# Attention chunks with one-bank accumulators, a third of the squares moved to ScalarE, and another order of the loads and copies around them

## The chip, the cores and the metric

The kernel runs on one core of one Trainium2 chip. The metric is the device time of one execution in microseconds, as the median of three runs. The engines are named as the profile names them: PE is the matrix engine (TensorE), PEld its weight loads, DVE is VectorE, ACT is ScalarE, POOL is GpSimd, SP is the engine that issues most of the DMAs.

## What is computed

```python
scores = (1.0 / S) * np.matmul(z, z.transpose(0, 2, 1))   # B=2, S=3008, d_qk=64
attn = np.maximum(scores, 0.0) ** 2
x = (u * np.matmul(attn, v)).reshape(B * S, D)            # D=256
for w_in, w_out in ((moe_w_in, moe_w_out), (moe2_w_in, moe2_w_out)):   # 256 -> 2048 -> 256
    h = x @ w_in
    g = h - np.tanh(h)      # first network
    # second network: g = h where h >= 1, 0 where h <= -1, (h + 1)**2 / 4 between
    x = g @ w_out
```

The weights come as 64-bit floats; u, v and z are 32-bit.

## The kernel before

Every product is made in three parts. A tile is kept as hi (the float rounded to the format that PE multiplies) and lo (what is left), and hi by hi, hi by lo and lo by hi are summed in PSUM.

**Attention.** For each batch the 3008 queries are cut into chunks of 512 columns (five, and a last one of 448), and the keys into 12 blocks of 256 (NPA). One step is one chunk and one block; there are 144 steps. In a step `attn_s` makes the scores on PE (6 matmuls into the tile `sc`, two banks), ACT takes them out with Relu and the factor 1/S (`r`, L260), DVE squares them in full precision (`a`, L267), ACT squares them rounded (`hi`, L268), and DVE subtracts (`lo`, L272). Two steps later (LAG) `attn_av` multiplies v by hi and lo: 24 matmuls, 20 in the last step of a chunk, in pairs of half the rows, h=0 and h=1, into two accumulators `acc[0]` and `acc[1]`. Each accumulator is a tile of two banks, one bank for each half d of the 256 columns of v, and the pool `ps_a` holds two such tiles, so that PSUM is full (`ps_s` has the other four banks). In the last step of a chunk the half d=0 is finished first: ACT copies `acc[0]`'s part to `y` (L309), DVE adds `acc[1]`'s (L310); then the same for d=1; at the end DVE multiplies by u (L315).

**Networks.** 12 chunks of 512 tokens, 8 blocks of 256 hidden columns each, twice. `ffn_s` makes 12 matmuls, ACT and DVE make g and split it, and two steps later `ffn_av` makes 12 more into an accumulator tile of two banks from `ps_a`. The last chunk of the second network is made untransposed and goes out by one ACT copy and one DMA.

**Loads.** z, v and the weights are loaded into four `raw` buffers, split into hi (ACT, L88) and lo (DVE, L91) and kept in a ring of 18 tiles; z is first transposed by DVE (L124). `pump(i)` issues the DMAs up to 14 steps ahead and the splits two steps ahead or when there is room. The weights are first turned from 64-bit to 32-bit floats by some seven DVE passes a tile (`convert`), dealt out by `make(i)` at CONVERT passes a step: 1.2 in the attention, 2.0 in the networks, and none in the first 12 steps and around the change of batch.

**Order.** The schedule is written out by hand: each engine works off its instructions in the order in which the code issues them, and waits only for the tiles that it reads or overwrites. The order of a step i is `pump(i)`, the hooks (u's loads and transposition), the scores and squares of step i, the deferred lo splits (`flush`), the product with v of step i-2, `make(i)`. So the copies y of a finished chunk, which belong to the product of step i-2, stand on ACT and DVE behind the squares of step i.

Of the kernel before, what the change touches and what calls it, by code (L numbers as in the profile page):

```python
# [15 lines left out]
P = 128  # L16
LAG = 2
GROUP = 1
# [5 lines left out]
CONVERT = (1.2, 2.0)  # L24
# [3 lines left out]
def attention_then_two_ffn(  # L28
# [15 lines left out]

    nc = tc.nc
# [8 lines left out]
    SCALE = 1.0 / S  # L54
# [12 lines left out]
    ps_a = ctx.enter_context(tc.tile_pool(name="ps_a", bufs=2, space=bass.MemoryType.PSUM))  # L67
# [33 lines left out]
    def load_z(b, g):  # L101
# [4 lines left out]
        def dma():  # L106
# [132 lines left out]
    accs = {}  # L239

    def attn_s(todo):

        got = []
        for b, c, t in todo:
            n = min(QT, S - QT * c)
            ps = ps_s.tile([P, 2, 512], F32, tag="s", name="sc")
            q = zs[b, c]
            for k, (x, y) in enumerate(((0, 0), (0, 1), (1, 0))):
                for j in range(2):
                    half = slice(64 * j, 64 * j + 64)  # L250
                    g, k0 = divmod((2 * t + j) * P, QT)
                    nc.tensor.matmul(  # L252
                        ps[:, j, :n], zs[b, g][half, x, k0 : k0 + P], q[half, y, :n], start=(k == 0), stop=(k == 2)
                    )
            got.append((ps, n))
        out = []
        for ps, n in got:
            s = (slice(None), slice(None), slice(0, n))
            r = tmp_p.tile([P, 2, 512], F32, tag="t1", name="r")
            nc.scalar.activation(out=r[s], in_=ps[s], func=AF.Relu, scale=SCALE)  # L260
            out.append((r, s, n))
        held = []
        for r, s, n in out:
            a = tmp_p.tile([P, 2, 512], F32, tag="t2", name="a")
            hi = sp_p.tile([P, 2, 512], F32R, tag="hi", name="hi")
            lo = sp_p.tile([P, 2, 512], F32R, tag="lo", name="lo")
            nc.vector.tensor_tensor(out=a[s], in0=r[s], in1=r[s], op=ALU.mult)  # L267
            nc.scalar.activation(out=hi[s], in_=r[s], func=AF.Square)  # L268
            held.append((hi, lo, n))
            got.append((a, s))  # L270
        for (a, s), (hi, lo, _) in zip(got[len(held):], held):
            nc.vector.tensor_tensor(out=lo[s], in0=a[s], in1=hi.bitcast(F32)[s], op=ALU.subtract)  # L272
        flush()
        return held

    def attn_av(b, c, t, hi, lo, n):
        if t == 0:
            accs[b, c] = [ps_a.tile([P, 2, 512], F32, tag="acc", name=f"acc{h}") for h in range(2)]
# [27 lines left out]
        for d in range(2):  # L306
            his(d)
            los(d)
            nc.scalar.activation(out=y[:, d, :n], in_=acc[0][:, d, :n], func=AF.Copy)  # L309
            nc.vector.tensor_tensor(out=y[:, d, :n], in0=y[:, d, :n], in1=acc[1][:, d, :n], op=ALU.add)  # L310
        o = 0
        while o < n:
            g, r = divmod(b * S + QT * c + o, 4 * P)
            k = min(n - o, 4 * P - r)
            nc.vector.tensor_tensor(  # L315
                out=xs[g][:, :, r : r + k], in0=y[:, :, o : o + k], in1=ut[:, :, o : o + k], op=ALU.mult
            )
            o += k
# [42 lines left out]
    def ffn_av(net, c, f, hi, lo, n):  # L361
        if f == 0:
            accs[net, c, "f"] = ps_a.tile([P, 2, 512], F32, tag="acc", name="acc")
# [221 lines left out]
```

## Time and profile before

| what | value |
|---|---|
| median of 3 runs | 1607.31 us (1605.94 to 1611.07) |
| the profiled execution | 1606.49 us |
| its span, first to last instruction | 1604.7 us |
| busy share of the span: PE, DVE, ACT | 96%, 71%, 48% |
| mean granted clock of PE | 0.98 of full speed |
| PE waiting for anything, by the list of waits | some 56 us, 41.5 of them for y (L309, L310) |

The share of busy time is a mean over stages with different limits: PE is busy without a break in the networks and has gaps in the attention. So the profile is read by stretches of the span, cut where chunks begin, then by what PE waited for, then as a timeline around a wait. A start in a timeline is where an instruction began, in us from the span's start; the bracket at the end of a row says how long the engine stood idle before it and which instruction let it go. The granted clock (PEclk) is 1.00 at 2.4 GHz and 0.50 at 1.2 GHz.

### The profile page before, as it was taken

The page shows a single profiled execution, that of the slowest core. Times are in us where ns is not written, and L with a number is a line of the kernel's source. Part 1 is how long each engine was busy: PE and PEld are TensorE (multiplying, and loading weights), DVE is VectorE, ACT ScalarE, POOL GpSimd, SP SyncE. Part 2 cuts the span into 40 slices and gives each one's busy share as a digit, 9 for nine tenths or more (in the row PEclk, how much of TensorE's full clock was granted, in tenths as well). Part 3 has the DMA queues.
Part 4 walks back from the last instruction along what each step waited for, and adds up shares of the span by engine and source line. Part 5 has one row for each costly group of instructions (what it writes and reads, how often), then busy time and mean ns, then how long its engine had stood idle before and what let it go on. Part 6 is the DMA issues. An engine that isn't in the chain of part 4 may idle for free.

```text
span 1604.7 us, 21195 instructions
## 1 busy us (share of the span) xinstructions
PE 1544.3 (96%) x8935; PEld 1300.1 (81%) x8935; DVE 1142.6 (71%) x1175; ACT 776.2 (48%) x806; POOL 0.7 (0%) x5
## 2 busy tenths in 40 slices
PE   7899999799999989999999999999999999999998
PEld 5677878688878868888888888898888888888888
DVE  6788888888888876666666544557776767767775
ACT  5555555655565744444444444445434344444443
POOL 0000000000000000000000000000000000000000
PEclk9899999899999999999999999999999999999999
DMA  4220223301211321111100000011000000000001
GB/s 108 57 60 21 54 56 76 86 17 41 57 35 46 104 72 40 40 40 40 37 23 27 33 1 0 14 30 37 13 13 14 14 14 13 12 4 13 14 14 24
DMA packets 146608, 56.70 MB, mean 35 GB/s; under 512 B 123600, under 2 KB 130128, under 8 KB 146512
## 3 DMA queue, kind: packets, MB, share of 16 engines
q1 hardware_dynamic: 146512, 55.34, 13.9%
q8 instruction: 70, 1.15, 0.3%
q14 instruction: 26, 0.21, 0.0%
HBM read 40.76 MB, written 14.55 MB: 34 GB/s over the span
## 4 chain that ended last, share of the span: by engine, by line
PE 89%; DVE 6%; ACT 2%; issue 1%; DMA 1%; SPq 1%; DVEq 0%
PE acc L370 31%; PE acc L287 21%; PE h L338 11%; PE h L340 11%; PE h L339 11%; PE sc L252 5%; DVE a L267 2%; DVE lo L272 1%; PE acc L403 1%; ACT r L260 1%; DMA zraw<-in_z_dram 1%; DVE y L310 1%; DVE v L91 1%; SPq L113 0%; DVE zt L124 0%
## 5 line engine op out<-in xcount | busy, mean ns | idle before, releaser
L287 PE MATMUL acc<-hi,v 64*128 64x512 f32 (+1 forms) x2256 | 328.9, 398 | 46.1 <-ACT y L309 27.1
L370 PE MATMUL acc<-gh,w_out 128*128 128x512 f32 (+1 forms) x1472 | 360.3, 387 | 0.0
L88 ACT ACTIVATE gh<-g 128x1024 fp32r<-128x1024 f32 (+1 forms) x192 | 200.4, 1044 | 267.6 <-DVE g L357 141.5
L287 PEld LDWEIGHTS acc<-hi,v 64*128 64x128 f32 x2256 | 253.1, 191 | 91.9 <-ACT y L309 32.8
L370 PEld LDWEIGHTS acc<-gh,w_out 128*128 128x128 f32 x1472 | 275.6, 188 | 54.7
L338 PE MATMUL h<-xl,w_in 128*128 128x512 f32 (+1 forms) x768 | 296.3, 386 | 0.0
L340 PE MATMUL h<-xh,w_in 128*128 128x512 f32 (+1 forms) x768 | 296.0, 385 | 0.0
L339 PE MATMUL h<-xh,w_in 128*128 128x512 f32 (+1 forms) x768 | 295.9, 385 | 0.0
L91 DVE TENSOR_TENSOR gl<-g,gh 128x1024 fp32r<-128x1024 f32 (+1 forms) x192 | 230.0, 1198 | 61.6 <-ACT gh L88 61.6
L349 DVE TENSOR_TENSOR g<-h,t 128x1024 f32<-128x1024 f32 (+1 forms) x96 | 115.4, 1203 | 149.5 <-ACT t L347 149.5
L352 DVE TENSOR_SCALAR t<-h 128x1024 f32<-128x1024 f32 (+1 forms) x96 | 115.4, 1203 | 142.1 <-PE h L340 142.1
L260 ACT ACTIVATE r<-sc 128x1024 f32<-128x1024 f32 (+1 forms) x144 | 145.0, 1007 | 144.3 <-PE sc L252 143.4
L370 PE MATMUL acc<-gl,w_out 128*128 128x512 f32 (+1 forms) x736 | 195.0, 387 | 0.0
L267 DVE TENSOR_TENSOR a<-r 128x1024 f32<-128x1024 f32 (+1 forms) x144 | 172.5, 1198 | 27.0 <-ACT r L260 26.0
L287 PE MATMUL acc<-lo,v 64*128 64x512 f32 (+1 forms) x1152 | 190.6, 392 | 0.5 <-DVE lo L272 0.5
L272 DVE TENSOR_TENSOR lo<-a,hi 128x1024 fp32r<-128x1024 f32 (+1 forms) x144 | 173.3, 1203 | 19.5 <-PE acc L287 1.0
L347 ACT ACTIVATE t<-h 128x1024 f32<-128x1024 f32 (+1 forms) x96 | 96.9, 1009 | 166.9 <-PE h L340 166.8
L355 ACT ACTIVATE t<-t 128x1024 f32<-128x1024 f32 (+1 forms) x96 | 100.3, 1045 | 156.5 <-DVE t L352 156.5
L338 PEld LDWEIGHTS h<-xl,w_in 128*128 128x128 f32 x768 | 144.6, 188 | 28.7 <-issue 0.6
L339 PEld LDWEIGHTS h<-xh,w_in 128*128 128x128 f32 x768 | 144.6, 188 | 27.7
L340 PEld LDWEIGHTS h<-xh,w_in 128*128 128x128 f32 x768 | 144.4, 188 | 27.5
L370 PEld LDWEIGHTS acc<-gl,w_out 128*128 128x128 f32 x736 | 137.9, 188 | 27.4
(52 smaller groups left out, 1078.2 us busy)
## 6 DMA issues: line engine op xcount, KB each, us to landing
wide_in<-in_moe_w_in_dram SPq DMA_DIRECT2D x16, 512.0 KB, 3.8
wide_out<-in_moe_w_out_dram SPq DMA_DIRECT2D x16, 512.0 KB, 3.9
vraw<-in_v_dram SPq DMA_DIRECT2D x22, 256.0 KB, 3.0
out_dram<-ot SPq DMA_DIRECT2D x88, 64.0 KB, 1.9
ub<-in_u_dram SPq DMA_DIRECT2D x80, 64.0 KB, 2.5
w_in<-m_in SPq DMA_DIRECT2D x16, 256.0 KB, 2.1
w_out<-m_out SPq DMA_DIRECT2D x16, 256.0 KB, 2.1
wraw_in<-w_in SPq DMA_DIRECT2D x16, 256.0 KB, 2.6
```

Source lines behind the costliest of these rows:

```text
L88: nc.scalar.activation(out=hi, in_=src, func=AF.Copy)
L91: nc.vector.tensor_tensor(out=lo, in0=src, in1=hi.bitcast(F32), op=ALU.subtract)
L260: nc.scalar.activation(out=r[s], in_=ps[s], func=AF.Relu, scale=SCALE)
L267: nc.vector.tensor_tensor(out=a[s], in0=r[s], in1=r[s], op=ALU.mult)
L272: nc.vector.tensor_tensor(out=lo[s], in0=a[s], in1=hi.bitcast(F32)[s], op=ALU.subtract)
L287: nc.tensor.matmul(acc[h][:, d, :n], lhsT, g[half, j, :n], start=start, stop=stop)
L338: nc.tensor.matmul(ps[:, j, :n], w[:, 0, k, fs], xl[:, k, :n], start=(k == 0), stop=False)
L339: nc.tensor.matmul(ps[:, j, :n], w[:, 1, k, fs], xh[:, k, :n], start=False, stop=False)
L340: nc.tensor.matmul(ps[:, j, :n], w[:, 0, k, fs], xh[:, k, :n], start=False, stop=(k == 1))
L349: nc.vector.tensor_tensor(out=g[s], in0=ps[s], in1=t1[s], op=ALU.subtract)
L352: nc.vector.tensor_scalar(out=t1[s], in0=ps[s], scalar1=1.0, scalar2=-1.0, op0=ALU.min, op1=ALU.max)
L370: nc.tensor.matmul(acc[:, d, :n], w[:, part, j, d * P : (d + 1) * P], g[:, j, :n], start=start, stop=stop)
```

## The change

The accumulators become tiles of one bank each: four for an attention chunk (`acc[d][h]`), two for a network chunk, out of a pool of four. The lo passes go to a list `tail` that is issued at the end of a step, behind the product with v and behind `make`; in step 1 of a chunk, which is the step in which the chunk before is finished, hi goes there too. In every third step (t % 3 == 2) the square `a` is made by ACT. The multiplication by u is deferred to the next step. The score factor leaves the Relu: z is scaled by 2**-6 when it is split, and the rest, squared, is applied with u. The conversion rate in the attention is 1.5 a step, with a longer pause around the change of batch and one around the end of the attention; the load splits are limited to one early step a time in the last chunk. At the start the loads of the first z go half to SP and half to ACT, only z is split before the first scores, and v's second block is loaded after the first step's scores are issued. The copies out of network accumulators are made bank by bank, the last one half on DVE and half on ACT with a DMA each.

```diff
-GROUP = 1
+ZEXP = 2.0**-6
...
-CONVERT = (1.2, 2.0)
+CONVERT = (1.5, 2.0)
...
-    SCALE = 1.0 / S
+    SCALE = (1.0 / S / ZEXP**2) ** 2
...
-    ps_a = ctx.enter_context(tc.tile_pool(name="ps_a", bufs=2, space=bass.MemoryType.PSUM))
+    ps_a = ctx.enter_context(tc.tile_pool(name="ps_a", bufs=4, space=bass.MemoryType.PSUM))
...
-        def dma():
+        def dma(other=nc.sync):
...
-                nc.sync.dma_start(
+                (other if i % 2 else nc.sync).dma_start(
...
-            split(w[:, 0, :], w[:, 1, :], zt, now=True)
+            nc.scalar.activation(out=w[:, 0, :], in_=zt, func=AF.Copy, scale=ZEXP)
+            nc.vector.scalar_tensor_tensor(
+                out=w[:, 1, :], in0=zt, scalar=ZEXP, in1=w[:, 0, :].bitcast(F32), op0=ALU.mult, op1=ALU.subtract
+            )
...
-            nc.scalar.activation(out=r[s], in_=ps[s], func=AF.Relu, scale=SCALE)
...
+    tail = []
...
+        nc.scalar.activation(out=r[s], in_=ps[s], func=AF.Relu)
+
+        def square_hi():
+            nc.scalar.activation(out=hi[s], in_=r[s], func=AF.Square)
+
+        if t % 3 == 2:
+            square_hi()
+            nc.scalar.activation(out=a[s], in_=r[s], func=AF.Square)
+        else:
             nc.vector.tensor_tensor(out=a[s], in0=r[s], in1=r[s], op=ALU.mult)
-            nc.scalar.activation(out=hi[s], in_=r[s], func=AF.Square)
-            held.append((hi, lo, n))
-            got.append((a, s))
-        for (a, s), (hi, lo, _) in zip(got[len(held):], held):
-            nc.vector.tensor_tensor(out=lo[s], in0=a[s], in1=hi.bitcast(F32)[s], op=ALU.subtract)
+
+            tail.append(square_hi) if t == 1 else square_hi()
         flush()
-        return held
+        tail.append(lambda: nc.vector.tensor_tensor(out=lo[s], in0=a[s], in1=hi.bitcast(F32)[s], op=ALU.subtract))
+        return hi, lo, n
...
-            accs[b, c] = [ps_a.tile([P, 2, 512], F32, tag="acc", name=f"acc{h}") for h in range(2)]
+            accs[b, c] = [[ps_a.tile([P, 512], F32, tag="acc", name=f"acc{d}{h}") for h in range(2)] for d in range(2)]
...
-                nc.tensor.matmul(acc[h][:, d, :n], lhsT, g[half, j, :n], start=start, stop=stop)
+                nc.tensor.matmul(acc[d][h][:, :n], lhsT, g[half, j, :n], start=start, stop=stop)
...
-            nc.scalar.activation(out=y[:, d, :n], in_=acc[0][:, d, :n], func=AF.Copy)
-            nc.vector.tensor_tensor(out=y[:, d, :n], in0=y[:, d, :n], in1=acc[1][:, d, :n], op=ALU.add)
-        o = 0
-        while o < n:
-            g, r = divmod(b * S + QT * c + o, 4 * P)
-            k = min(n - o, 4 * P - r)
-            nc.vector.tensor_tensor(
-                out=xs[g][:, :, r : r + k], in0=y[:, :, o : o + k], in1=ut[:, :, o : o + k], op=ALU.mult
-            )
-            o += k
+            nc.scalar.activation(out=y[:, d, :n], in_=acc[d][0][:, :n], func=AF.Copy)
+            nc.vector.tensor_tensor(out=y[:, d, :n], in0=y[:, d, :n], in1=acc[d][1][:, :n], op=ALU.add)
+
+        def scaled():
+            o = 0
+            while o < n:
+                g, r = divmod(b * S + QT * c + o, 4 * P)
+                k = min(n - o, 4 * P - r)
+                nc.vector.scalar_tensor_tensor(
+                    out=xs[g][:, :, r : r + k], in0=y[:, :, o : o + k], scalar=SCALE, in1=ut[:, :, o : o + k],
+                    op0=ALU.mult, op1=ALU.mult,
+                )
+                o += k
+
+        deferred.append(scaled)
...
-                nc.scalar.activation(out=xs[c], in_=acc[:, :, :n], func=AF.Copy)
+                for d in range(2):
+                    nc.scalar.activation(out=xs[c][:, d, :], in_=acc[d][:, :n], func=AF.Copy)
...
+                for d in range(2):
+                    nc.vector.transpose(out=o[:, d].rearrange("p c e -> p (c e)"), in_=acc[d])
...
+        for i, (t0, k) in enumerate(((0, min(2, nt)), (2, nt - 2))):
+            if k <= 0:
+                continue
+            src = acc[i][:, : k * D].rearrange("p (t d) -> p t d", d=D)
+            if i:
+                nc.scalar.activation(out=o[:, t0 : t0 + k, :], in_=src, func=AF.Copy)
+                nc.scalar.dma_start(out=to[:, t0 : t0 + k, :], in_=o[:, t0 : t0 + k, :])
+            else:
+                nc.vector.tensor_copy(out=o[:, t0 : t0 + k, :], in_=src)
+                nc.sync.dma_start(out=to[:, t0 : t0 + k, :], in_=o[:, t0 : t0 + k, :])
...
-                if i > 5 and ld in staged and ld["at"] < i - 1 and n < 2:
+                if i > 5 and ld in staged and ld["at"] < i - 1 and n < (1 if NATT - NPA <= i < NATT else 2):
...
+        first[0]["steps"][0][0](nc.scalar)
+        first[1]["steps"][0][0]()
+        warm(WARM)
+        first[0]["steps"][1][0]()
...
-        warm(WARM)
-        for ld in first:
-            ld["steps"][1][0]()
...
-        flush()
...
+        pauses = ((0, NPA), (NPA * QC - 9, NPA * QC + 13), (NATT - 5, NATT + 1))
...
+            if not any(a <= i < e for a, e in pauses):
+                state["credit"] += CONVERT[0] if i < NATT else CONVERT[1]
...
+        def second(i):
+            if i >= LAG:
+                _, av_fn, args = pairs[i - LAG]
+                av_fn(*args, *held.pop(i - LAG))
...
+            if i == LAG:
+                second(i)
...
-            for i in group:
-                if i >= LAG:
-                    _, av_fn, args = pairs[i - LAG]
-                    av_fn(*args, *held.pop(i - LAG))
-                make(i)
+            if i == 0:
+                first[1]["steps"][1][0]()
+                first[2]["steps"][0][0]()
+            elif i == 1:
+                first[2]["steps"][1][0]()
+            if i != LAG:
+                second(i)
+            make(i)
+            for fn in tail:
+                fn()
+            tail.clear()
 
 
 # ---- launch: one core; inputs and outputs as the reference has them ----
```

Three places show how rows move. First ACT and DVE where the first chunk of batch 0 ends: acc is the finished accumulator, e and m are conversion steps, x is the product with u; of the two r's the later one is of step 1 of the next chunk. ACT before, then after:

```order
L260 ACTIVATE r_684<-sc_677 128x1024
L268 ACTIVATE hi_687<-r_684 128x1024
L260 ACTIVATE r_728<-sc_721 128x1024
L268 ACTIVATE hi_731<-r_728 128x1024
L309 ACTIVATE y_736<-acc0_208 128x512 x2
L260 ACTIVATE r_770<-sc_763 128x1024
L268 ACTIVATE hi_773<-r_770 128x1024
```

```order
L264 ACTIVATE r_689<-sc_679 128x1024
L267 ACTIVATE hi_687<-r_689 128x1024
L264 ACTIVATE r_733<-sc_723 128x1024
L313 ACTIVATE y_736<-acc00_191 128x512
L313 ACTIVATE y_736<-acc10_193 128x512
L267 ACTIVATE hi_731<-r_733 128x1024
L264 ACTIVATE r_775<-sc_765 128x1024
L267 ACTIVATE hi_773<-r_775 128x1024
L271 ACTIVATE a_772<-r_775 128x1024
```

The two y copies stand ahead of hi_731 now, and the next step has a third pass, a_772. DVE at the same place, before, then after:

```order
L267 TENSOR_TENSOR a_686<-r_684 128x1024
L272 TENSOR_TENSOR lo_688<-a_686,hi_687 128x1024
L192 TENSOR_SCALAR e0_in_0_719<-wide0_in_0_716 128x512
L267 TENSOR_TENSOR a_730<-r_728 128x1024
L272 TENSOR_TENSOR lo_732<-a_730,hi_731 128x1024
L310 TENSOR_TENSOR y_736<-y_736,acc1_209 128x512 x2
L315 TENSOR_TENSOR x0_90<-y_736,ut0_0_589 128x1024
```

```order
L273 TENSOR_TENSOR a_686<-r_689 128x1024
L197 TENSOR_SCALAR e0_in_0_720<-wide0_in_0_717 128x512
L277 TENSOR_TENSOR lo_688<-a_686,hi_687 128x1024
L273 TENSOR_TENSOR a_730<-r_733 128x1024
L314 TENSOR_TENSOR y_736<-y_736,acc01_192 128x512
L314 TENSOR_TENSOR y_736<-y_736,acc11_194 128x512
L199 TENSOR_SCALAR m0_in_0_719<-wide0_in_0_717 128x512
L203 TENSOR_SCALAR e0_in_0_720<-e0_in_0_720 128x512
L277 TENSOR_TENSOR lo_732<-a_730,hi_731 128x1024
L321 SCALAR_TENSOR_TENSOR x0_90<-y_736,ut0_0_591 128x1024
```

The additions stand directly behind a_730, and lo_732 behind them and two conversion steps. Second, the start on ACT, before, then after (z0_0, v0_0: batch 0, first tile):

```order
L88 ACTIVATE z0_0_125<-zt0_0_123 128x512
L88 ACTIVATE v0_0_128<-vraw0_0_111 128x512
L88 ACTIVATE v0_1_130<-vraw0_1_113 128x512
L88 ACTIVATE z0_1_150<-zt0_1_148 128x512
L260 ACTIVATE r_160<-sc_153 128x1024
L268 ACTIVATE hi_163<-r_160 128x1024
L260 ACTIVATE r_177<-sc_170 128x1024
L268 ACTIVATE hi_180<-r_177 128x1024
```

```order
L115 DMA zraw0_0_106<-in_z_dram 32x16x32 x2
L128 ACT_TABLE_LOAD
L128 ACTIVATE z0_0_123<-zt0_0_121 128x512
L128 ACTIVATE z0_1_142<-zt0_1_140 128x512
L264 ACTIVATE r_155<-sc_145 128x1024
L267 ACTIVATE hi_153<-r_155 128x1024
L90 ACTIVATE v0_0_159<-vraw0_0_111 128x512
L264 ACTIVATE r_176<-sc_166 128x1024
L90 ACTIVATE v0_1_180<-vraw0_1_161 128x512
L267 ACTIVATE hi_174<-r_176 128x1024
```

The first r has no v ahead of it any more, and the second hi has v0_1 ahead of it. SP issues that v0_1 (vraw0_1) before, then after:

```order
L113 DMA zraw0_0_106<-in_z_dram 32x16x32 x4
L139 DMA vraw0_0_111<-in_v_dram 128x2x256
L139 DMA vraw0_1_113<-in_v_dram 128x2x256
L113 DMA zraw0_1_134<-in_z_dram 32x16x32 x4
L139 DMA vraw0_2_139<-in_v_dram 128x2x256
```

```order
L115 DMA zraw0_0_106<-in_z_dram 32x16x32 x2
L144 DMA vraw0_0_111<-in_v_dram 128x2x256
L115 DMA zraw0_1_126<-in_z_dram 32x16x32 x4
L144 DMA vraw0_2_131<-in_v_dram 128x2x256
L144 DMA vraw0_3_133<-in_v_dram 128x2x256
L115 DMA zraw0_2_135<-in_z_dram 32x16x32 x4
L144 DMA vraw0_1_161<-in_v_dram 128x2x256
```

Its issue has moved behind two v blocks and the third z.

## Rows read from the trace of the kernel before

**Rows 1.** Stretches: length; busy us and instructions of PE, PEld, DVE, ACT, POOL; PEclk, DMA, GB/s.

```profile
0.00:67.15 67.15, 52.65 (x365) 38.47 (x366) 49.74 (x55) 40.48 (x50) 0.73 (x5) 0.90 0.44 99
67.15:247.49 180.34, 168.90 (x1424) 141.53 (x1425) 153.45 (x167) 104.30 (x104) 0.00 (x0) 0.98 0.19 45
158.54:203.18 44.64, 41.71 (x357) 36.86 (x357) 38.82 (x43) 26.19 (x26) 0.00 (x0) 1.00 0.20 48
247.49:342.09 94.60, 81.54 (x712) 72.13 (x712) 81.13 (x93) 58.97 (x72) 0.00 (x0) 0.95 0.28 63
342.09:526.14 184.05, 173.41 (x1425) 151.16 (x1425) 153.42 (x171) 104.28 (x104) 0.00 (x0) 0.94 0.17 42
526.14:583.19 57.05, 50.67 (x391) 43.12 (x391) 48.15 (x64) 32.07 (x41) 0.00 (x0) 0.91 0.35 101
583.19:1604.70 1021.51, 1017.09 (x4621) 853.68 (x4619) 656.68 (x629) 436.06 (x435) 0.00 (x0) 1.00 0.08 22
```

**Rows 2.** What PE waited for: us in total, times, longest us.

```profile
PE acc L287 <- ACT y L309: 27.1, 12, 6.7
PE acc L287 <- DVE y L310: 14.4, 14, 2.1
```

**Rows 3.** Chain of waits, pace of PE (attention, then first network): start, us, what.

```profile
211.13 2.72 PE acc L287 x24
...
616.00 2.72 PE acc L370 x12
```

**Rows 4.** Timeline at one chunk boundary: start, us, engine, line, out<-in, [idle before].

```profile
155.89 1.03 ACT L260 ACTIVATE r<-sc 128x1024 f32<-128x1024 f32 x1 [1.28 <-PE sc L252]
156.15 0.83 PE L287 MATMUL acc<-lo,v 64*128 64x512 f32 x4
156.95 1.06 ACT L268 ACTIVATE hi<-r 128x1024 fp32r<-128x1024 f32 x1
156.95 1.23 DVE L267 TENSOR_TENSOR a<-r 128x1024 f32<-128x1024 f32 x1 [0.48 <-ACT r L260]
157.91 0.58 ACT L309 ACTIVATE y<-acc 128x512 f32<-128x512 f32 x1
158.31 1.23 DVE L272 TENSOR_TENSOR lo<-a,hi 128x1024 fp32r<-128x1024 f32 x1
158.54 0.50 PE L287 MATMUL acc<-hi,v 64*128 64x512 f32 x1 [1.56 <-ACT y L309]
159.45 0.68 DVE L310 TENSOR_TENSOR y<-y,acc 128x512 f32<-128x512 f32 x1
160.19 0.96 PE L287 MATMUL acc<-hi,v 64*128 64x512 f32 x5 [1.15 <-DVE y L310]
```

**Rows 5.** Timeline where batch 0 gives way to batch 1.

```profile
250.01 0.98 PE L252 MATMUL sc<-z,z 64*128 64x448 f32 x6
...
288.62 0.70 DVE L124 STREAM_TRANSPOSE zt<-zraw 128x512 f32<-128x512 f32 x1
289.36 0.63 ACT L88 ACTIVATE z<-zt 128x512 fp32r<-128x512 f32 x1 [3.47 <-DVE zt L124]
289.90 1.01 ACT L260 ACTIVATE r<-sc 128x1024 f32<-128x1024 f32 x1
294.94 0.53 ACT L309 ACTIVATE y<-acc 128x448 f32<-128x448 f32 x1
297.68 0.62 DVE L310 TENSOR_TENSOR y<-y,acc 128x448 f32<-128x448 f32 x1
301.29 0.91 PE L287 MATMUL acc<-hi,v 64*128 64x512 f32 x3
```

**Rows 6.** Timeline where attention gives way to the first network.

```profile
575.67 0.53 ACT L309 ACTIVATE y<-acc 128x448 f32<-128x448 f32 x1
576.25 2.14 PE L287 MATMUL acc<-hi,v 64*128 64x448 f32 x6 [5.30 <-ACT y L309]
```

**Rows 7.** Timeline of the start.

```profile
0.74 1.97 SPq L113 DMA_DIRECT2D zraw<-in_z_dram  x4
9.46 0.63 ACT L88 ACTIVATE z<-zt 128x512 fp32r<-128x512 f32 x1 [1.68 <-DVE zt L124]
10.00 1.00 ACT L260 ACTIVATE r<-sc 128x1024 f32<-128x1024 f32 x1
12.15 2.08 PE L287 MATMUL acc<-hi,v 64*128 64x512 f32 x8
...
46.87 0.71 DVE L124 STREAM_TRANSPOSE zt<-zraw 128x512 f32<-128x512 f32 x1 [3.10 <-DMA zraw<-in_z_dram]
```

**Rows 8.** DMA issues of 0 to 70 us: KB each, median us to landing.

```profile
vraw<-in_v_dram SPq DMA_DIRECT2D x11, 256.0 KB, 3.1
```

**Rows 9.** Timeline of the end.

```profile
1600.31 0.81 ACT L418 ACTIVATE o<-acc 128x768 f32<-128x768 f32 x1 [2.64 <-PE acc L403]
```

More of the change, by code (lines that the diff above doesn't have):

```diff
@@ new lines, in attention_then_two_ffn, with attn_s @@
+    tail = []
+    def attn_s(b, c, t):
+        n = min(QT, S - QT * c)
+        ps = ps_s.tile([P, 2, 512], F32, tag="s", name="sc")
+        q = zs[b, c]
+        for k, (x, y) in enumerate(((0, 0), (0, 1), (1, 0))):
+            for j in range(2):
+                half = slice(64 * j, 64 * j + 64)
+                g, k0 = divmod((2 * t + j) * P, QT)
+                nc.tensor.matmul(
+                    ps[:, j, :n], zs[b, g][half, x, k0 : k0 + P], q[half, y, :n], start=(k == 0), stop=(k == 2)
+                )
+        s = (slice(None), slice(None), slice(0, n))
+        a = tmp_p.tile([P, 2, 512], F32, tag="t2", name="a")
+        hi = sp_p.tile([P, 2, 512], F32R, tag="hi", name="hi")
+        lo = sp_p.tile([P, 2, 512], F32R, tag="lo", name="lo")
+        r = tmp_p.tile([P, 2, 512], F32, tag="t1", name="r")
+        nc.scalar.activation(out=r[s], in_=ps[s], func=AF.Relu)
[5 more added lines that the diff above has]
+        else:
+            nc.vector.tensor_tensor(out=a[s], in0=r[s], in1=r[s], op=ALU.mult)
+            tail.append(square_hi) if t == 1 else square_hi()
@@ L362, in ffn_av @@
         if f == 0:
-            accs[net, c, "f"] = ps_a.tile([P, 2, 512], F32, tag="acc", name="acc")
+            accs[net, c, "f"] = [ps_a.tile([P, 512], F32, tag="acc", name=f"acc{d}") for d in range(2)]
         acc = accs[net, c, "f"]
@@ L370, in mm @@
                 nc.tensor.matmul(
-                    acc[:, d, :n], w[:, part, j, d * P : (d + 1) * P], g[:, j, :n], start=start, stop=stop
+                    acc[d][:, :n], w[:, part, j, d * P : (d + 1) * P], g[:, j, :n], start=start, stop=stop
                 )
@@ L403, in mm2 @@
             nc.tensor.matmul(
-                acc4[:, tt, :], g[:, j, tt * P : (tt + 1) * P], w[:, part, j, :],
+                acc[tt // 2][:, tt % 2 * D : (tt % 2 + 1) * D], g[:, j, tt * P : (tt + 1) * P], w[:, part, j, :],
                 start=start, stop=stop, skip_group_check=True,
@@ L446, in attention_then_two_ffn @@
             for t in range(NPA):
-                pairs.append((None, attn_av, (b, c, t)))
+                pairs.append((attn_s, attn_av, (b, c, t)))
     for net, (wi, wo) in enumerate(((w_in1, w_out1), (w_in2, w_out2))):
@@ L465, in warm @@
     def warm(n):
-        ps = ps_a.tile([P, 2, 512], F32, tag="acc", name="warm")
+        ps = ps_a.tile([P, 512], F32, tag="acc", name="warm")
         for i in range(n):
-            nc.tensor.matmul(ps[:, 0, :], zero[:, :P], zero, start=True, stop=True)
+            nc.tensor.matmul(ps, zero[:, :P], zero, start=True, stop=True)
     with tc.manual_schedule():
@@ L528, in make @@
                     state["step"] = 1
-        begin = NPA
-        change = (NPA * QC - 6, NPA * QC + 10)
-        NATT = B * QC * NPA
-        order = [range(i, i + GROUP) for i in range(0, NATT, GROUP)]
-        order += [range(i, i + 1) for i in range(NATT, len(pairs) + LAG)]
-        for group in order:
-            for i in group:
-                pump(i)
-                for fn, args in hooks.get(i, ()):
-                    fn(*args)
-            i = group[0]
-            if i < NATT:
-                held.update(zip(group, attn_s([pairs[i][2] for i in group])))
-            elif i < len(pairs):
+        def second(i):
+            if i >= LAG:
+                _, av_fn, args = pairs[i - LAG]
+                av_fn(*args, *held.pop(i - LAG))
+        for i in range(len(pairs) + LAG):
+            pump(i)
+            for fn, args in hooks.get(i, ()):
+                fn(*args)
+            if i == LAG:
+                second(i)
+            if i < len(pairs):
                 s_fn, _, args = pairs[i]
```

39 lines of the change are left out of this document (3 added, 36 removed).

## The prediction

> **What bounds the kernel now.** I read the stretches first [rows 1]. From 583.19 us on the two networks keep PE busy for 1017.09 of 1021.51 us at clock 1.00: nothing is to be had there, and nothing in that stretch may get worse. All that the change can win lies in the attention, before 583.19. PE's pace there is 2.72 us for 24 matmuls of 512 columns, 0.1133 each; in the network 2.72 for 12, so 0.2267 each [rows 3]; a 448-column one I estimate by its columns at 0.0992. One chunk has 144/12 = 12 steps of 6 + 24 matmuls, less 4 in the last step: 356. That is 40.35 us at full pace, or 35.3 for a chunk of 448 columns. The stretches took more:
>
> Eight ordinary chunks, 67.15 to 247.49 and 342.09 to 526.14: 180.34 + 184.05 = 364.4 us against 8 x 40.35 = 322.8, so 41.6 lost. The stretch with the change of batch: 94.60 against 40.35 + 35.3 = 75.65, so 19.0 lost. The hand-over, 526.14 to 583.19: 10 matmuls of 512 columns, 344 of 448 and 36 of the network make 1.1 + 34.1 + 8.2 = 43.4 against 57.05, so 13.6 lost. Together 74.
>
> The list of PE's waits says where: 27.1 us for the ACT copy y (L309) and 14.4 for the DVE addition y (L310) [rows 2]. One boundary shows how [rows 4]. The lo matmuls of half d=0 end at 156.98. The copy of that half would be free to run, but stands behind hi, which ACT began at 156.95, so it runs from 157.91. The next PE matmul, of the other half, writes another bank of the same tile and stands until 158.54 (1.56 us); the second accumulator waits for the addition, which stands behind a and lo on DVE, until 160.19 (1.15 more). The rest of the 74 is mostly clock: the granted clock is 0.98 over the first four ordinary chunks and 0.94 over the other four [rows 1], that is 180.34 x 0.02 x 2 = 7 and 184.05 x 0.06 x 2 = 22 us at 1.2 GHz, half of each lost. One chunk with the same two waits, 158.54 to 203.18, shows 1.00 and still took 44.64, so the waits alone are worth about 4.3 a boundary (a wait also costs the pipeline's restart).
>
> **The change, part by part.** *One-bank accumulators, emptied ahead of the next squares.* The second half's matmuls no longer touch a tile that ACT and DVE read. ACT now has r, y, y, hi, and DVE a, y, y, then conversion steps and lo. By the boundary's rows [rows 4]: r ends at 156.92, y(0) can run 157.0 to 157.6 and y(1) from the end of its half, 10 x 0.1133 later, 158.1 to 158.7. DVE ends a at 158.18 and adds y(0) until 158.9. PE goes on without a stop: 1.13 for the other half until 158.1, 0.68 for the scores until 158.8, and there the second matmul of the next chunk needs the addition of 158.9. I charge 0.5 for each of the ten ordinary boundaries (a wait near 0.2 and the restart); the bounds are 0 and, if DVE is one pass later, 1.5. What is queued behind the y's: hi starts at 158.7 instead of 156.95, its lo two conversion steps later, near 161.5; the matmuls that read them come a whole step (3.4 us) after the scores of 158.8, so from 162.2. Then r of the next step starts 0.7 late and is done 4 us before its bank is wanted. Covered. The eight ordinary chunks: 41.6 becomes 8 x 0.5 = 4, so **-37.6**; with the waits gone I let the clock losses go too (rival 1).
>
> *Every third square on ScalarE.* 4 passes of a chunk's 12 go from DVE (1.23) to ACT (hi, the same function and shape: 1.06) [rows 4]. Per ordinary chunk DVE was busy 153.45/4 = 38.4 us and becomes 38.4 - 4.9 + 2.4 (12 x 0.3 more conversion steps, each bounded by a half-width pass, 0.68) = 35.9 of 41; ACT 104.30/4 = 26.1 + 4.2 = 30.3. A step with the square on ACT asks 1.03 + 1.06 + 1.06 = 3.2 of ACT, under PE's 3.4. Both fit, so it costs nothing by itself. Against this part speaks the Trainium skill, "ScalarE: Activation LUTs", section "Rules for kernel authors": it gives a multiplication to VectorE and calls it up to about 3 times faster there in bf16. The two rows, in f32, differ the other way, so the sum goes by them; by the rule it would be rival 5.
>
> *Change of batch.* Here the last chunk of batch 0 also splits the z and v of batch 1, and both queues are full. I walked them in the new order at the durations of the rows: a saved DVE pass is answered by an ACT pass, and z's transposition comes near 287.6 instead of 288.62 [rows 5]. From there the order is z 0.63, r 1.01, hi 1.06, two v (0.63 each), r 1.0, y, y; the addition stands behind a and two v on DVE. That puts the addition's end at 287.6 + 0.7 + 0.65 + 1.0 + 1.05 + 1.25 + 1.0 + 1.25 + 1.25 + 0.6 = 296.35 and the first matmuls of batch 1 there, instead of 301.29: -4.9. PE still idles there some 5 us, so I expect a stretch at 1.2 GHz after it, 3.4 to 6.8 us, of which the stretch of before spent most while idle: +2.5. ACT's z and v passes go on: +0.6. The two ordinary waits at the ends of this stretch go: -3.1, less 0.5. Sum **-4.4** (bounds +2 and -11).
>
> *Hand-over.* Before, y(0) was behind w, w, t and gh on ACT and began at 575.67; PE waited 5.30 for it [rows 6], at clock 0.91 over the stretch. Now the last attention matmuls need no y. The first to need one are those of the first network step, behind 20 x 0.0992 + 12 x 0.2267 = 4.7 us of PE work after the second h. The chain that must fit into it is t, g, gh, y, y: 1.03 + 1.23 + 1.06 + 0.53 + 0.62 = 4.5 [rows 4 to 6]. It just fits: 13.6 becomes 0.7, **-12.9**; if ACT is as late at t as before, 3 to 4 of it come back. The conversions are paused and the loads slowed in these steps; they are far enough ahead (1.5 conversion steps in each of 105 steps make 157, and the first network's 16 weight tiles need 7 each, 112).
>
> *First loads on two queues.* Four z loads took 1.97 us of issue [rows 7]; two of them on ACT save 1 us at the first scores. Then ACT no longer has two v ahead of r: r near 8.3 instead of 10.00. But v's second block is now issued only when the first has been split on DVE, near 13.7, and lands 3.1 later [rows 8]; on ACT the second hi stands behind it, so the second step is some 5 us later than before. The loop of z loads, which paces this chunk, is shorter by the lo that moved behind v, about 0.6 a turn, and the last z arrives near 47.8 against 46.87 [rows 7], while the v behind it is split earlier. From there PE runs at its own pace. I take **-0.5** for the start, bounds -2.5 and +8.
>
> *Score factor on z and x; FFN accumulators.* The same passes with a scalar more, on tiles of the same size: 0. The network's copies are split in two on engines that are busy 436 and 657 of 1021 us [rows 1]: 0. The last copy, 0.81 on ACT [rows 9], goes half to DVE, ahead of PE's end: **-0.5**.
>
> Sum: -37.6 - 4.4 - 12.9 - 0.5 - 0.5 = -55.9. The profiled execution took 1606.49 (span 1604.7 and 1.8 around it), the median is 1607.31, 0.8 above: 1606.49 - 55.9 + 0.8 = **1551**.
>
> **The rivals.** (1) The clock stays low at the boundaries. For: with the same waits some boundaries dropped it and some did not. Against: 1021 us of unbroken work at 1.00 [rows 1]. 7 + 22 us at half stay: +14, 1565. Chance 0.10. (2) The addition is late: DVE carries more conversion steps, and if they push it by a pass, ten boundaries wait 1.5 and keep half of the clock loss: 10 x 1.5 + 7 = 22, 1573. 0.12. (3) The start: the late v is not made good, +8: 1559. 0.12. (4) The change doesn't do what it says, and the second half still waits for the first's y: only hand-over and batch change gain, 1589. 0.02. (5) The moved square is dearer on ACT than hi. At three times DVE's 1.23, 3.7 us, an ordinary chunk still fits (26.1 + 14.8 = 40.9 of 41), but the two fuller stretches lose some 10 each: 1571. Against it stands hi's 1.06 [rows 4]. 0.02. The page's rule above points this way. (6) Slower: ACT becomes the bound of every step. Three steps have seven full passes in 10.2 us of PE. From 1.46 a pass ACT sets the pace, and at 1.63 the 48 triples lose 48 x (7 x 1.63 - 10.2) = 58, all that is won; beyond that it is slower, near 1615. The rows show 1.03 and 1.06. 0.05, of which 0.02 near the point of no change. The forecast keeps 0.57.
>
> **How the numbers follow.** The forecast's own bounds are 1539 (no boundary wait, -11 at the batch, start -2.5, in part) and 1563. The range takes in rivals 1, 2, 3 and 5, so 1539 to 1575. Differences under 0.3% (5 us) can't be told from no change. Rivals 1 to 5 and the forecast are faster, 0.95; rival 6 gives 0.02 for no change and 0.03 for slower.
>
> **What would show it.** Ordinary chunks of about 40.9 us at clock 1.00, no wait of PE for y above 0.5 except at the batch change, where one of about 5 us stands before the first matmuls of batch 1; y on ACT directly behind r; the network's stretch still 1021. It is wrong if PE waits for lo or r in steady steps, or if the granted clock stays under 1.00 in chunks that have no wait.

## The result, and the profile after

The changed kernel took 1543.75 us (1543.56 to 1544.73) against 1607.12 (1605.94 to 1611.07): 0.960 of the time, 95% interval 0.959 to 0.962. The prediction was 1551, range 1539 to 1575. The profiled execution took 1543.72, its span is 1541.6. Timed again beside the experiments, the kernel before took 1611.1 to 1612.9 in the median and the changed kernel 1544.92, so the gain lies between 63 and 68 us; where an experiment is set against the kernel before, it is against the runs beside it.

The stretches, cut at the same places as [rows 1] (0.63 us behind the first copy y of a boundary; columns as there):

```profile
0.00:63.21 63.21, 51.59 (x373) 38.00 (x375) 42.77 (x50) 42.87 (x53) 0.73 (x5) 1.00 0.45 103
63.21:226.62 163.41, 162.47 (x1425) 133.23 (x1423) 137.74 (x165) 119.37 (x120) 0.00 (x0) 1.00 0.23 59
226.62:313.54 86.92, 81.47 (x718) 70.43 (x716) 68.86 (x79) 65.83 (x80) 0.00 (x0) 0.96 0.29 63
313.54:475.83 162.29, 162.18 (x1424) 133.03 (x1422) 136.90 (x168) 119.33 (x120) 0.00 (x0) 1.00 0.23 58
475.83:520.56 44.73, 44.73 (x386) 39.03 (x382) 36.85 (x48) 34.92 (x44) 0.00 (x0) 1.00 0.37 105
520.56:1541.60 1021.04, 1017.08 (x4621) 853.34 (x4619) 655.79 (x634) 436.88 (x449) 0.00 (x0) 1.00 0.08 21
```

Against [rows 1]: start -3.9, the eight ordinary chunks -16.9 and -21.8, change of batch -7.7, hand-over -12.3, networks -0.5; together -63.1. In the fourth and fifth lines PE is busy almost without a gap at clock 1.00.

PE's waits for y, which answer to [rows 2] (us in total, times, longest):

```profile
PE acc L291 <- DVE y L314: 2.9, 2, 2.1
PE acc L291 <- ACT y L313: 2.5, 1, 2.5
```

41.5 us for y have become 5.4, of which 4.6 stand at the change of batch and 0.86 at the first boundary; at the other nine boundaries and the hand-over this list has none. One of these boundaries, which answers to [rows 4] (timeline, columns as there; the first row is the product with v of an ordinary step, and PEld are the weight loads):

```profile
180.64 2.20 PE L291 MATMUL acc<-hi,v 64*128 64x512 f32 x16
...
184.46 1.03 ACT L264 ACTIVATE r<-sc 128x1024 f32<-128x1024 f32 x1 [1.28 <-PE sc L256]
...
185.42 0.60 ACT L313 ACTIVATE y<-acc 128x512 f32<-128x512 f32 x1
185.52 1.22 DVE L273 TENSOR_TENSOR a<-r 128x1024 f32<-128x1024 f32 x1 [0.44 <-ACT r L264]
...
186.31 1.06 PE L256 MATMUL sc<-z,z 64*128 64x512 f32 x6
186.51 0.60 ACT L313 ACTIVATE y<-acc 128x512 f32<-128x512 f32 x1 [0.48 <-PE acc L291]
186.66 1.28 DVE L314 TENSOR_TENSOR y<-y,acc 128x512 f32<-128x512 f32 x2
...
186.99 2.52 PE L291 MATMUL acc<-hi,v 64*128 64x512 f32 x16
187.00 1.05 ACT L267 ACTIVATE hi<-r 128x1024 fp32r<-128x1024 f32 x1
187.40 1.68 PEld L291 LDWEIGHTS acc<-hi,v 64*128 64x128 f32 x15 [0.45 <-DVE y L314]
```

y stands directly behind r, and PE goes from the second half through the scores into the next chunk. There a short wait is left that the list does not show: the second matmul's weight load stands 0.45 us until the first addition ends, near 187.3 (186.66 and half of 1.28), and the 16 matmuls take 2.52 where those of an ordinary step take 2.20. So some 0.3 us a boundary are still waited for y.

### The profile page after: what moved, and what is told of

Its sections match the earlier page's. It is cut to its first block, busy times and chain, and to the rows that moved or that the text cites. A ratio compares the mean times of both kernels' runs of the same rounds, so it can differ in the third digit from the quotient of the medians.

```text
span 1541.6 us, 21242 instructions
## 1 busy us (share of the span) xinstructions
PE 1519.5 (99%) x8935; PEld 1267.1 (82%) x8935; DVE 1078.9 (70%) x1139; ACT 819.2 (53%) x866; POOL 0.7 (0%) x5
## 4 chain that ended last, share of the span: by engine, by line
PE 93%; DVE 2%; ACT 2%; issue 1%; DMA 1%; SPq 1%; DVEq 0%
PE acc L379 32%; PE acc L291 21%; PE h L347 11%; PE h L348 11%; PE h L349 11%; PE sc L256 5%; PE acc L411 1%; ACT r L264 1%; DVE lo L277 1%; DVE a L273 1%; DMA zraw<-in_z_dram 1%; ACT hi L267 1%; SPq L115 0%; DVE zt L126 0%; ACT z L128 0%
## 5 line engine op out<-in xcount | busy, mean ns | idle before, releaser
L291 PE MATMUL acc<-hi,v 64*128 64x512 f32 (+1 forms) x2256 | 314.7, 388 | 12.0 <-DVE v L93 4.6
L291 PEld LDWEIGHTS acc<-hi,v 64*128 64x128 f32 x2256 | 238.0, 186 | 58.9 <-DVE y L314 7.2
L291 PE MATMUL acc<-lo,v 64*128 64x512 f32 (+1 forms) x1152 | 184.5, 385 | 0.3 <-DVE lo L277 0.2
L267 ACT ACTIVATE hi<-r 128x1024 fp32r<-128x1024 f32 (+1 forms) x144 | 150.2, 1043 | 4.2
```

The lines of the kernel that those rows point to most:

```text
L291: nc.tensor.matmul(acc[d][h][:, :n], lhsT, g[half, j, :n], start=start, stop=stop)
```

## Experiments

The changed kernel itself was run once more beside the later ones:

> The changed kernel once more, unchanged, beside the two others of this call, since the differences looked at are 2 to 8 us: 1543 to 1545, first copy y near 62.6.

It gave 1544.92 (1543.77 to 1545.98), first y at 63.77 in place of 62.58 (first y is where the first copy y begins on ACT, and so tells how long the start took). Differences of about 1 us in the start therefore show nothing by themselves.

**Banks or order.** one_bank: the kernel before with one-bank accumulators, in attention and networks, and nothing else. One line of its edit:

```diff
...
-            accs[b, c] = [ps_a.tile([P, 2, 512], ...) for h in range(2)]
+            accs[b, c] = [[ps_a.tile([P, 512], ...) for h in range(2)] for d in range(2)]
...
```

> The kernel before with one-bank accumulators alone (four for an attention chunk, two for a network chunk; copies out of network accumulators bank by bank); order, squares, loads and rates as before. Theory: of the two waits of a boundary, 1.56 us for the copy and 1.15 for the addition, the first goes and 1.2 stays, so some 15 us are won directly, up to 30 with clock, the hand-over's 5.30 us wait partly: 1577 to 1592. Rival A (the order alone matters): no gain, 1603 to 1609. Rival C (the banks alone matter): most of the 63 us, 1545 to 1560.

1566.31 (1564.55 to 1566.63) against 1612.37: 46 won, more than the theory gave and short of rival C. The wait that was to stay did stay. One boundary (timeline):

```profile
152.43 1.06 ACT L268 ACTIVATE hi<-r 128x1024 fp32r<-128x1024 f32 x1
...
153.40 1.06 ACT L309 ACTIVATE y<-acc 128x512 f32<-128x512 f32 x2
153.79 1.23 DVE L272 TENSOR_TENSOR lo<-a,hi 128x1024 fp32r<-128x1024 f32 x1
...
154.93 1.28 DVE L310 TENSOR_TENSOR y<-y,acc 128x512 f32<-128x512 f32 x2
...
155.66 1.20 PE L287 MATMUL acc<-hi,v 64*128 64x512 f32 x8 [1.14 <-DVE y L310]
```

What I had too small: PE's waits for y fell from 41.5 to 17.2 us, 24 in place of my 15, since the hand-over gained with the chunks (57.05 to 46.70 us); and the ordinary chunks got nearly all of their clock back: with this one stop of 1.14 a boundary, seven of the eight ordinary chunks show 1.00. two_bank is the changed kernel without the banks:

```diff
-            accs[b, c] = [[ps_a.tile([P, 512], ...) for h in range(2)] for d in range(2)]
+            two = [ps_a.tile([P, 2, 512], ...) for h in range(2)]
+            accs[b, c] = [[two[h][:, d, :] for h in range(2)] for d in range(2)]
```

> The changed kernel with its accumulators as two-bank tiles again (two of them for an attention chunk, one for a network chunk); the new order of squares and copies stays. Theory (both the banks and the order are needed): at an ordinary boundary PE stands again between the halves, about 0.65 us for y(0) on ACT and 1.2 us for its addition, which stands behind a on DVE, and some 1 us more before the next chunk's first accumulation. That is 2.5 to 3 us a boundary, as much as the kernel before lost by its two waits, and the granted clock should fall under 1.00 in some chunks again: ten boundaries and the hand-over give 1570 to 1590. Rival A (the order alone did it, since y no longer stands behind hi): 1544 to 1552, waits for y under 1 us in all. Rival B (the banks are not what PE waits on; the gain is from the moved squares and pauses): 1544 as well, so old_order has to tell A from B.

1583.41 (1582.6 to 1584.04), as the theory said. One boundary, and the chunk ahead of it (stretch, columns as above):

```profile
152.17 0.49 PE L292 MATMUL acc<-hi,v 64*128 64x512 f32 x1 [0.55 <-ACT y L314]
...
153.47 1.28 PE L292 MATMUL acc<-hi,v 64*128 64x512 f32 x5 [0.81 <-DVE y L315]
```

```profile
108.00:152.10 44.10, 42.76 (x356) 39.78 (x356) 34.53 (x42) 29.91 (x30) 0.00 (x0) 0.96 0.20 49
```

Five of the eight ordinary chunks show this clock. old_order is the changed kernel without the order:

```diff
-            tail.append(square_hi) if t == 1 else square_hi()
+            square_hi()
+        nc.vector.tensor_tensor(out=lo[s], in0=a[s], in1=hi...)
         flush()
-        tail.append(lambda: ... lo ...)
```

> The changed kernel with the old order of the squares: hi at once in every step, lo directly behind it, so that at a boundary the copies y stand behind hi on ACT, and the additions behind a and lo on DVE; one-bank accumulators, moved squares, pauses and start stay. Theory (both are needed): PE does the other half and the scores without a stop, about 1.8 us, and then waits for the addition, which comes about 3.2 us after the end of the first half: 1.2 to 1.4 us a boundary, ten times, with a part of the clock lost: 1556 to 1574. Rival A (the order alone did it): all of what was won at the boundaries comes back, 1580 or more. Rival C (the banks alone did it, and the order is worth nothing): 1544 to 1547, no wait for y over 0.5.

1572.59 (1568.69 to 1573.34). At the boundaries the theory held (13.0 us of waits for the addition, ten of them 1.0 to 1.7), but it was slower than one_bank, whose order it shares: the start alone took 6 us more (below). By the starts of the copy y, an ordinary chunk took 45.5 us before, 43.9 in two_bank (all but the banks), 42.2 in one_bank (the banks alone), 42.5 in old_order (all but the order), 40.7 with everything. So the banks are worth 3.2 to 3.3 and the order 1.5 to 1.8 on top of them; neither does it alone. The Trainium skill, "Perfetto Trace Analysis", section "Matmuls", wants independent matmul groups to rotate through different PSUM banks, so that emptying one overlaps the next. Here that was not enough: the kernel before had its two halves in different banks of one tile and PE stood 1.56 us at the boundary [rows 4]; with a tile to each bank the two overlap. What PE waited for was the tile.

**The moved squares.** dve_squares has all squares on DVE:

```diff
-        if t % 3 == 2:
+        if t < 0:
```

> The changed kernel with every square a on DVE again; all else stays. Theory (neither engine sets the pace of an ordinary step, the move is worth nothing there): DVE goes from 34 to some 37 us busy in a chunk of 40.6, no wait of PE for lo or y in ordinary chunks; a few us at most at the start, the change of batch and the hand-over: 1542 to 1549. It may even win at the change of batch, where lo stands behind the square that ACT makes. Rival D (the square that moved is what keeps DVE ahead of the additions, and is where the 7.5 us came from that the forecast missed): waits for y or lo at every boundary, 1551 to 1565.

1546.72 (1546.65 to 1547.16), 2 to 3 above the changed kernel. Chunks take 40.8, and PE's list has no wait at boundaries but the first; about half of the loss or more is in the start (first y at 64.72). act_squares has 11 of 12 on ACT:

```diff
-        if t % 3 == 2:
+        if t != 1:
```

> The changed kernel with every square a on ACT but that of a chunk's second step: 11 of 12 instead of 4. From the trace of the changed kernel a chunk of 40.6 us has 29.7 us of ACT; 7 more squares of 1.04 make 37.0. Theory (an ordinary step of r, hi and a, 3.1 us, still fits into PE's 3.4, so the move costs nothing in ordinary chunks whatever the number; the fuller stretches, start, change of batch, hand-over, lose some us): ordinary chunks 40.6 to 41.2, 1545 to 1560. Rival 6 of the prediction (ACT sets the pace of the steps): chunks over 42 and PE waiting for r or lo in steady steps, 1560 to 1600.

1552.45 (1551.97 to 1553.12). Three ordinary chunks of the second batch (stretch, columns as above):

```profile
361.60:483.50 121.90, 121.82 (x1072) 99.96 (x1070) 79.50 (x105) 109.28 (x112) 0.00 (x0) 1.00 0.23 59
```

40.63 a chunk with ACT busy 90%: rival 6 has no footing. The 8 us are lost where splits are added, at the start (first y 67.37) and the change of batch (90.4 for 86.9). A moved square took 1.04 us on ACT where DVE's takes 1.22 (128x1024, f32). The rule of the Trainium skill ("ScalarE: Activation LUTs", section "Rules for kernel authors") gives multiplications to VectorE, with a factor that it states for bf16; for this f32 square the two engines came out the other way.

**The start.** old_start is the changed kernel with the first loads as before:

```diff
-        first[0]["steps"][0][0](nc.scalar)
-        first[1]["steps"][0][0]()
+        for ld in first:
+            ld["steps"][0][0]()
         warm(WARM)
-        first[0]["steps"][1][0]()
         for ld in first:
+            ld["steps"][1][0]()
             live.append(ld["last"])
+        flush()
...
-            if i == 0: ...                       # the later first loads
```

> The changed kernel with the start of the kernel before: the first three loads (z, and v's first two blocks) all issued at once on SP, all split ahead of the first scores. The traces so far: the first copy y on ACT begins at 66.52 us in the kernel before, 62.58 in the changed one, 67.06 with the old start and old order, and 73.18 with the new start and the old order (old_order). So the new start by itself cost 6 us there. Theory S (the new order shortened the start, since lo now stands behind the splits of v and z, and the two queues add 1 us at most): the first y between 61 and 64, the whole 1542 to 1546. Rival S2 (the two queues and the single first split won the 3.9 us that the start gave): the first y near 66.5, the whole 1547 to 1549.

1541.74 (1541.51 to 1543.25), first y at 61.74: theory S, and the new start even costs 2 to 3 us of the whole. The four starts together: old start and old order 67.06 (one_bank), new start and old order 73.18 (old_order), old start and new order 61.74, both new 62.58. The new start is a loss in either order, by 6.1, or by 0.8 to 2.0 (62.58 and 63.77, the two runs of the changed kernel); the order gains 5.3 or some 10. (one_bank differs from old_start in the moved squares too, 1 to 2 of this.) Where the new start loses, in the changed kernel on SP and ACT:

```profile
7.25 1.92 SPq L115 DMA_DIRECT2D zraw<-in_z_dram  x4
13.25 8.51 SPq L144 DMA_DIRECT2D vraw<-in_v_dram  x3
...
15.87 0.63 ACT L90 ACTIVATE v<-vraw 128x512 fp32r<-128x512 f32 x1 [4.55 <-DMA vraw<-in_v_dram]
```

v's second block is issued behind two other v blocks and the z loads, which hold the four buffers. early_v issued it right behind the first:

```diff
         first[1]["steps"][0][0]()
+        first[2]["steps"][0][0]()
         warm(WARM)
...
                 first[1]["steps"][1][0]()
-                first[2]["steps"][0][0]()
```

> The changed kernel with v's second block issued right behind the first at the start, in place of after the first split (the four raw buffers stay, so z's second tile takes the fourth, and the later loads wait for a buffer). Theory (ACT stood idle 4.55 us for this transfer, with hi of the second step behind it, and PE waited 1.98 for the split at 21.37): 2 to 4 us won, 1540 to 1542. Rival (the loop of z loads, which ends at 46.15 us with PE waiting 2.50 for the Relu behind it, paces the first chunk whatever comes before; the third z then gets its buffer later): 1543 to 1548.

1544.19 (1543.9 to 1544.84): nothing. The wait at 21.37 went, and the one before the Relu grew from 2.50 to 3.33. That another load now lacked a buffer is what raw6 tests:

```diff
-    raw_p = ctx.enter_context(tc.tile_pool(name="raw", bufs=4))
+    raw_p = ctx.enter_context(tc.tile_pool(name="raw", bufs=6))
```

> The changed kernel with six raw load buffers instead of four, and nothing else. Theory (four buffers hold the loads back at the start: v's second block was issued at 13.25 us only, when the first had been split and its buffer was free, and the last z landed at 46.15 with PE waiting 2.50 behind it): the second v goes out some 2 to 3 us earlier, the first copy y on ACT near 59 instead of 62.6 to 63.8, the change of batch unchanged since PE waits there for y and not for a load: 1539 to 1542. Rival (the buffers helped in best only because the old start and the other order at the change of batch made the loads the last to come): 1543 to 1545.

1541.49 (1540.88 to 1541.61), 2.3 and 3.4 less than the two runs of the changed kernel, first y at 59.39, and the last z is transposed at 42.98 in place of 46.15: the buffers it was.

**Hand-over and change of batch.** old_rates:

```diff
-CONVERT = (1.5, 2.0)
+CONVERT = (1.2, 2.0)
...
-                if i > 5 and ... and n < (1 if NATT - NPA <= i < NATT else 2):
+                if i > 5 and ... and n < 2:
...
-        pauses = ((0, NPA), (NPA * QC - 9, NPA * QC + 13), (NATT - 5, NATT + 1))
+        pauses = ((0, NPA), (NPA * QC - 6, NPA * QC + 10))
```

> The changed kernel with the old rates alone: 1.2 conversion passes a step in the attention, the shorter pause around the change of batch, no pause and no slower loads around the hand-over. Theory (the one-bank tiles took PE off y at the hand-over, and the chain t, g, gh, y, y fits before the first network accumulation with nothing to spare: the additions end at 520.64, the accumulation starts at 520.56): with w splits again between them on ACT and DVE, y comes 1 to 4 us late, 1545 to 1548, with a wait for y at the first network accumulation. Rival (the pauses have no part in it): 1543 to 1545 and no such wait. At the change of batch conversion passes in three more steps may cost another 0 to 2.

1544.63 (1544.42 to 1545.77): the theory fell. PE's list has no wait at the hand-over, which took 45.04 us, as in the second run of the changed kernel. The other runs say what did it: 57.05 before, 53.99 in two_bank, 46.70 in one_bank, 45.22 in old_order. So it was the tiles, and the order has little part in it. batch_order:

```diff
+            late = i in (NPA * QC, NPA * QC + 1)
+            if not late: pump(i)                 # else behind second(i)
-            pump(i)
...
-        if t % 3 == 2:
+        if t % 3 == 2 and not (b == 0 and c == QC - 1 and t == NPA - 1):
...
+            tail.append(square) if (b, c, t) == (1, 0, 1) else square()
```

> The changed kernel with another order at the change of batch alone: in the first two steps of batch 1 the loads' splits come behind the product with v instead of ahead of the scores, the last square of batch 0 is on DVE, and the square of batch 1's second step stands behind the additions y. Theory (PE's idle 5 us there come from y standing behind r, which stands behind z's split, which waits for the transposition behind lo, and from the additions standing behind a and two v on DVE): the scores of the third step start some 1 us later (266.7), but the addition ends near 268.5 instead of 271.8: 2 to 4 us won, 1539.5 to 1542; under 1539 if the stretch at half clock goes too. Rival (z's second tile is then the last to come, and PE waits as long for it at the scores): 1543 to 1546.

What it goes at, in the changed kernel:

```profile
263.41 0.70 DVE L126 STREAM_TRANSPOSE zt<-zraw 128x512 f32<-128x512 f32 x1
264.15 0.63 ACT L128 ACTIVATE z<-zt 128x512 fp32r<-128x512 f32 x1 [1.78 <-DVE zt L126]
264.69 1.00 ACT L264 ACTIVATE r<-sc 128x1024 f32<-128x1024 f32 x1
...
268.63 0.97 ACT L313 ACTIVATE y<-acc 128x448 f32<-128x448 f32 x2
...
269.22 0.49 PE L291 MATMUL acc<-hi,v 64*128 64x512 f32 x1 [2.51 <-ACT y L313]
...
271.11 1.15 DVE L314 TENSOR_TENSOR y<-y,acc 128x448 f32<-128x448 f32 x2
...
271.78 1.65 PE L291 MATMUL acc<-hi,v 64*128 64x512 f32 x6 [2.07 <-DVE y L314]
```

And in batch_order:

```profile
268.47 0.50 PE L295 MATMUL acc<-hi,v 64*128 64x512 f32 x1 [1.40 <-ACT y L317]
269.52 2.10 PE L295 MATMUL acc<-hi,v 64*128 64x512 f32 x15 [0.55 <-DVE y L318]
...
285.44 1.65 PE L256 MATMUL sc<-z,z 64*128 64x512 f32 x6 [2.71 <-ACT r L264]
```

The waits for y shrank from 4.6 to 1.95, as foreseen, and a new one of 2.71 took their place: 1542.91 (1541.59 to 1544.52), between theory and rival. The r it waited for stood behind a z, whose loads SP issued at 276.14 in place of 271.26, behind two v loads that took 6.95 us to issue and another gap of 2.6.

**A faster version.** best is old_start, batch_order and raw6 together, with no edit of its own.

> The changed kernel with the old start (worth 2.0 in old_start), the order of batch_order at the change of batch, and six raw load buffers instead of four, which is what batch_order's new wait (2.71 us at 285.44, behind a z load that SP issued 4.9 us later than in the changed kernel, after 7 us of waiting for a buffer) and the first chunk's z loads point to. Theory (the buffers hold the loads back): no wait of PE over 1 us at the change of batch but the one for y near 1.4 and 0.6; the first copy y before 60 in place of 62.58: 1533 to 1540. Rival (the splits on ACT and DVE, and not the buffers, pace the loads): 1540 to 1542.5, as old_start and batch_order alone, first y at 61 to 63.

1535.32 (1534.86 to 1535.68), 9.6 less than the changed kernel beside it, and 0.952 of the kernel before (0.951 to 0.954). Start and change of batch:

```profile
0.00:57.89 57.89, 49.62 (x373) 36.98 (x375) 42.52 (x50) 43.07 (x53) 0.73 (x5) 0.94 0.49 112
...
221.32:304.77 83.45, 81.02 (x715) 74.97 (x713) 69.41 (x80) 64.74 (x79) 0.00 (x0) 0.98 0.30 65
```

63.21 became 57.89 and 86.92 became 83.45; the 2.71 us wait is gone, which speaks for the buffers there too (best differs from batch_order in the start as well), while 1.40 and 0.55 for y stay.

## Why the prediction was right, point by point

**Ordinary boundaries** (-37.6): -38.7. The walk from [rows 4] held, in its small wait too: I charged 0.5 a boundary, and 0.3 is what the addition still costs there (2.52 us against 2.20 above), so that a chunk takes 40.6 to 40.7 where the pace gives 40.35. The steps between take 3.40, the pace itself. Rivals 1 and 2 fell: clock 1.00, and the addition late by no more than that 0.3, but for the first boundary's 0.86. That the clock losses went with the waits was assumed; the runs bear it out: of the eight ordinary chunks six lost clock before, five in two_bank, two in old_order, one in one_bank and none in the changed kernel.

**Moved squares** (0): 2 to 3 won (dve_squares), mostly in the start, where I had not looked for them. Rival 5 fell with 1.04 us a square. **Factor, copies, end** (-0.5): the networks' stretch gave -0.5.

**Hand-over** (-12.9): -12.3. "It just fits" was right; PE did not stop:

```profile
518.93 0.96 ACT L313 ACTIVATE y<-acc 128x448 f32<-128x448 f32 x2
...
519.49 1.15 DVE L314 TENSOR_TENSOR y<-y,acc 128x448 f32<-128x448 f32 x2 [1.56 <-ACT y L313]
...
520.56 1.98 PE L379 MATMUL acc<-gh,w_out 128*128 128x512 f32 x8
```

The pauses and slowed loads that I named beside it have no part in it (old_rates).

**Change of batch** (-4.4): -7.7. The walk from z's transposition to the end of the first addition, where PE goes on, took 8.37 us (263.41 to 271.78) against my 8.75, and the stretch at 1.2 GHz came as well: from 269.6 to 276.8 the granted clock was 0.53, and PE worked from 271.78 on. The failed step is the walk's beginning. Counted from the cut, I put the transposition at 40.1 (287.6 less 247.49) and it came at 36.8; the boundary wait booked apart explains 1.3 of that. The remaining 2 are DVE's. Counted from the first scores of that chunk, ahead of the boundary's waits, the transposition came after 47.95 us before, 45.95 in one_bank, 45.34 in old_order, 43.44 in old_rates and 42.79 in the changed kernel. So the banks alone gave 2.0, the longer pause of the conversions, which I left out there, 0.65, and the order 2.55, of which 1.01 is old_order's stop at the boundary and some 1.5 are left for DVE. Where these can come from: before, a step of the last chunk took 2.82 us there (columns as in the timelines):

```profile
284.19 1.09 DVE L272 TENSOR_TENSOR lo<-a,hi 128x896 fp32r<-128x896 f32 x1
285.19 0.69 DVE L91 TENSOR_TENSOR v<-vraw,v 128x512 fp32r<-128x512 f32 x1
285.80 1.08 DVE L267 TENSOR_TENSOR a<-r 128x896 f32<-128x896 f32 x1
287.01 1.09 DVE L272 TENSOR_TENSOR lo<-a,hi 128x896 fp32r<-128x896 f32 x1
```

and in dve_squares, with the same passes in the new order, 2.61:

```profile
262.43 1.08 DVE L277 TENSOR_TENSOR lo<-a,hi 128x896 fp32r<-128x896 f32 x1
263.43 1.08 DVE L273 TENSOR_TENSOR a<-r 128x896 f32<-128x896 f32 x1
264.43 0.68 DVE L93 TENSOR_TENSOR v<-vraw,v 128x512 fp32r<-128x512 f32 x1
265.04 1.08 DVE L277 TENSOR_TENSOR lo<-a,hi 128x896 fp32r<-128x896 f32 x1
```

lo right behind the a that it reads starts 1.21 after it; v there starts 1.00 after it. That is 0.21 a step, up to 2.5 us in the twelve steps of a chunk where DVE sets the time. I took the order of lo as free of cost.

**Start** (-0.5): -3.9, inside no bound of mine (-2.5 to +8), and for another reason than I gave. The two queues and the late v lose (old_start). In the z loop the late v cost 2.65 us up to the third z (18.62 against 15.97), and the three turns after it are 1.0 to 1.3 shorter where I saw 0.6, so that the last z came at 46.15 and not at my 47.8 ([rows 7] has 46.87):

```profile
46.15 0.71 DVE L126 STREAM_TRANSPOSE zt<-zraw 128x512 f32<-128x512 f32 x1 [2.41 <-DMA zraw<-in_z_dram]
```

The larger part, 3.2, was won behind that z, where I had PE at its own pace in both kernels: 19.65 us to the first y before, at clock 0.83 and with DVE busy for 18.01 of them, and 16.43 after, at 1.00. The second run of the changed kernel had the low clock too, 0.81, and took 17.62. So some 1.2 of it are the clock, which stayed up there in one run of the changed kernel and fell in the other, and 2.0 the rest; lo behind the splits and the moved squares are in it, and no run separates them there. Rival 3 was real: with the old order the late v cost 6.1.

So the forecast was 7 us too high, nearly all in the two stretches (-3.4 start, -3.3 change of batch) where DVE and the loads set much of the time and my terms took their order as nearly free.

## What to carry to other kernels

When a copy out of PSUM stands in PE's way, give each half a tile of its own, not only a bank, and put the copy ahead of the next work on its engine: here the tiles alone left a third of what was won in a chunk, and everything but the tiles two thirds. A list of waits can hide a short one: look at the weight loads and at the length of the first row behind a boundary too. Ask of every reordering what it does to loads that share buffers; early_v gained nothing and batch_order less than hoped, both with another load or wait taking the place of the one removed, and two more buffers gave 2.3 to 3.4 us alone.

## What the runs showed of the hardware

A DVE pass that reads what the one ahead of it wrote starts 0.2 us later than another would (rows above); no run separated the dependence from the kinds of passes. One stop of PE of 1.14 to 1.18 us a boundary left the clock at 1.00 in seven of eight chunks (one_bank; the eighth followed a stop of 1.80 and shows 0.96). In old_order the chunks behind its two longest ordinary stops, 1.68 and 1.55, show 0.96 and the six others, behind 1.14 to 1.33, 1.00. Two shorter stops with one matmul between them, 0.52 to 0.55 and 0.80 to 0.83, went with 0.96 in five chunks of two_bank and with 1.00 in a sixth, and one behind 0.73 and 1.67 shows 1.00 too. What decides there stays open.
